# A new hand-written step list for the first two chunks of attention plus feed-forward on one NeuronCore

## The chip, the cores and the metric

The kernel runs on 1 core of a Trainium2 chip. The metric is the device time of one execution in microseconds (us); the median of 3 runs before the change is 620.47 (620.06 to 621.1). Engines are named as in the profile: PE (TensorE matmul), PEld (its weight loads), DVE (VectorE), ACT (ScalarE), POOL (GpSimd), SP (SyncE, which here issues all DMAs).

## The reference

```python
B, H, S, D = 4, 8, 768, 64; block, window = 32, 16; scale = 1 / sqrt(D)
k_sum = k.reshape(B, H, 24, 32, D).max(axis=3)
v_sum = v.reshape(B, H, 24, 32, D).mean(axis=3)
scores_l = where(|i - j| < window, scale * q @ k.T, -1e9)
scores_s = scale * q @ k_sum.T + log(block)
a = softmax(concat([scores_l, scores_s]))          # sum + 1e-9 in the denominator
x = (a @ concat([v, v_sum])) as (3072 tokens, 512)
out = square(relu(x @ w_in)) @ w_out               # w_in 512x2048, w_out 2048x512, float64 words
```

Each query sees 31 neighbours and 24 block summaries (largest key, mean value). The weights arrive as 64-bit floats and are made into 32-bit ones on the chip.

## The kernel before, in words

**Tiling.** 3072 tokens are 24 groups of 128 (six per batch entry) and 12 chunks of two groups. The 2048 hidden columns are 16 f tiles. Matmuls of the feed-forward use a reduced 32-bit format, and each operand is split into a high and a low part, so that one product is three matmuls (high x high, high x low, low x high).

**Two regimes.** Chunks 2 to 11 run through `slot`, a fixed pipeline over pairs of f tiles with attention of the next groups placed between. Chunks 0 and 1 run from `START`, a string of about 600 steps in one order, in which weights are still arriving and being converted. Each engine takes its own steps from that string in that order and waits where an operand is not ready; nothing reorders within an engine. The list ends with S7, and the first slot's matmul follows on PE.

**The steps** (number: group, f tile or unit; a suffix a, v or p names the engine ACT, DVE or POOL):

- L: a DMA. `kv` transposed keys of batch 0, `kw` transposed keys and values of batch 1, `q`, `k`, `v` per group, `w` a weight tile of 1 MB, `vn` plain values for the block means.
- KS, KT, VT: block maxima and means (DVE). PK: copies the key summaries behind a group's gathered keys (DVE). SV, VC: means of batch 0 by PE, copied into place.
- S g.half: scores (PE); TT g.head: scale, mask, maximum (DVE); E: exponential (ACT); NR g.half: `inverse`, two tiny DVE instructions; N: `norm` (DVE or POOL); T g.half: four transposes on PE; TC: their copy out; O g: `outputs`, weights times values (PE); XH and XL: high (ACT) and low part (DVE) of the result.
- HI (ACT), LO (ACT or DVE), SH (DVE), AD (POOL): from 64-bit words to a float; CA: its high part (ACT or DVE); SU: its low part (DVE or POOL).
- F1: 12 matmuls of 256 columns; RE: relu; SQ: high part of the square (ACT); MU, GL: square and its low part (DVE); F2: 6 matmuls of 512 columns; EV: eviction of an accumulated output.

**Order of chunks.** `units` lists the FFN work of the first regime as 32 units of one chunk and one f tile: chunk 0 with f 0 to 4, chunk 1 with f 0 to 10, chunk 0 with f 5 to 15, chunk 1 with f 11 to 15.

**Buffers.** Six PSUM banks: scores in 0 and 1 for groups below 6; `free` is a queue of banks 3, 4 and 5 for T and F1; O of groups 0 to 4 always uses bank 2 (`outputs`). SBUF has 17 rooms of 8 KB per partition (`room`), shared by raw weights, split weights, `vn` and the key tiles: 16 split tiles end up in 16 of them, and one is spare.

**Scores.** Groups 0 to 3 use `scores_kt` (transposed keys in SBUF, 8 matmuls for a pair of heads), the later ones `scores` (gathered keys with the summaries behind them, 4 matmuls).

Of the kernel before, what the change touches and what calls it, by code (L numbers as in the profile page):

```python
# [45 lines left out]
TC1.0a L:q4 VC1v HI0 L:q3 VC2v LO0a N1.1p TT2.1 O0 TT2.2 TT2.0 HI2 SH0 T1.1 LO2v XH0a AD0 TC1.1v E2.1 XL0v E2.0
TT2.6 HI3 O1 TT2.5 SH2 CA0a SH3 AD2 TT2.7 XH1a TT2.4 TT2.3 E2.7 XL1v E2.2 S3.0 SU0v CA2a S3.1 LO3v E2.3 F1.0
L:w8 E2.4 L:k4 SU2v E2.6 L:w6 F1.1 E2.5 AD3 NR2.0 RE0v HI4 NR2.1 F1.2 MU0 RE1v SQ0 N2.1p SQ1 GL0v RE2a MU1 F2.0
SQ2 CA3v LO4a GL1v SU3p L:w9 T2.1 MU2 L:v2 HI8 F2.1 TT3.6 L:w7 TT3.4 TT3.5 L:v3 TT3.7 E3.6 GL2v L:k5 E3.7 N2.0v
F1.3 L:q5 E3.5 SH4 L:w5 E3.4 SH8 T2.0 TC2.1a F2.2 AD4 RE3v TC2.0a NR3.1 SQ3 MU3 HI6 GL3v TT3.1 F2.3 N3.1p TT3.2  # L50
# [21 lines left out]
def attn_ffn_kernel(ctx: ExitStack, tc: tile.TileContext, q, k, kt, v, vt, v0, w, masks, ident, mean, out):  # L72
# [46 lines left out]
    def load_k(g):  # L119
        nc.sync.dma_start(out=k_sb[g % 2][:, 0:4], in_=k[g // NT, g % NT])  # L120
# [553 lines left out]
```

## Time and profile before

| what | value |
|---|---|
| median of 3 runs | 620.47 us (620.06 to 621.1) |
| the profiled execution | 621.07 us, span 619.3 us |
| PE, DVE, ACT, POOL busy | 96%, 63%, 44%, 16% of the span |
| mean granted clock of PE | 0.992 |
| end of the step list (first matmul of chunk 2) | 138.45 us |

A row of a timeline gives start and duration in us, engine, source line, operation, tiles, shapes and count, and in brackets the idle time before it with what ended it. "x8" stands for fp32 matmuls counted in two passes each. A row of stretches gives the stretch, its length, and then busy us and count of each engine.

### The profile page before, as it was taken

To read this page: it belongs to the slowest core of one execution; us is meant where nothing else is said; L and a number is where in the kernel's file an instruction comes from. 1 tells how busy PE (TensorE), PEld (TensorE's weight loads), DVE (VectorE), ACT (ScalarE), POOL (GpSimd) and SP (SyncE) were. 2 spreads that over 40 slices of the span, in tenths; PEclk is the share of its full clock that TensorE was granted. 3 is DMA by queue.
4 is the path that set the end of the run, shared out by engine and by line. 5 is a ranking of instruction groups with operands and counts; after the bars stand their busy time and mean duration, and the time that the engine had idled before them with its cause. 6 is when DMAs were issued, how large, how long until landed. Compare 5 with 4: busy or idle time off the path is not lost.

```text
span 619.3 us, 12979 instructions
## 1 busy us (share of the span) xinstructions
PE 596.7 (96%) x5216; PEld 538.7 (87%) x5216; DVE 391.9 (63%) x1073; ACT 270.3 (44%) x706; POOL 97.2 (16%) x83
## 2 busy tenths in 40 slices
...
GB/s 302 380 351 327 214 62 15 195 155 166 0 2 130 143 2 114 109 1 106 116 2 78 144 52 49 174 1 22 150 2 2 171 0 3 86 1 1 35 0 35
DMA packets 19852, 60.36 MB, mean 97 GB/s; under 512 B 2768, under 2 KB 2896, under 8 KB 17744
## 3 DMA queue, kind: packets, MB, share of 16 engines
...
q14 instruction: 19, 0.16, 0.1%
...
## 4 chain that ended last, share of the span: by engine, by line
PE 92%; DMA 3%; DVE 2%; ACT 1%; SPq 1%; issue 0%; POOL 0%; DVEq 0%; POOLq 0%
PE o_ps L398 42%; PE ph L357 40%; PE s_ps L249 3%; PE ph L327 3%; PE s_ps L357 2%; DMA w_raw<-in_w 2%; DMA q_sb<-in_q 1%; PE ph L306 1%; PE s_ps L265 1%; PE s_ps L327 1%; DVE w_sb L234 0%; PE o_ps L136 0%; ACT w_sb L113 0%; SPq L159 0%; SPq L117 0%
## 5 line engine op out<-in xcount | busy, mean ns | idle before, releaser
L357 PE MATMUL ph<-xh,w_sb 128*128 128x256 f32 x1448 | 256.2, 279 | 0.7 <-DVE xl L344 0.5
L398 PE MATMUL o_ps<-w_sb,gh 128*128 128x512 f32 x768 | 237.9, 391 | 0.0
L357 PEld LDWEIGHTS ph<-xh,w_sb 128*128 128x128 f32 x1448 | 225.8, 189 | 9.1 <-issue 1.6
L357 PE MATMUL ph<-xl,w_sb 128*128 128x256 f32 x724 | 201.2, 278 | 0.0
L398 PEld LDWEIGHTS o_ps<-w_sb,gh 128*128 128x128 f32 x768 | 137.1, 188 | 24.9 <-issue 0.2
L376 DVE TENSOR_TENSOR ph<-ph,r 128x512 f32<-128x512 f32 (+1 forms) x101 | 64.7, 642 | 143.4 <-ACT r L365 142.7
L398 PE MATMUL o_ps<-w_sb,gl 128*128 128x512 f32 x384 | 151.4, 394 | 0.8 <-DVE gl L379 0.8
L365 ACT ACTIVATE r<-ph 128x512 f32<-128x512 f32 (+1 forms) x91 | 51.7, 568 | 199.0 <-PE ph L357 198.8
L357 PEld LDWEIGHTS ph<-xl,w_sb 128*128 128x128 f32 x724 | 136.9, 189 | 0.0
L285 ACT ACTIVATE e_sb<-e_sb,nmx 128x120 f32<-128x120 f32 x192 | 73.7, 385 | 78.2 <-DVE nmx L277 78.2
L313 DVE STREAM_TRANSPOSE pT<-e_sb 32x256 f32<-32x256 f32 x216 | 94.1, 436 | 3.7 <-POOL e_sb L300 0.7
L300 POOL TENSOR_TENSOR e_sb<-e_sb,sm 128x480 f32<-128x480 f32 x43 | 43.3, 1011 | 324.8 <-DVE sm L295 179.4
L398 PEld LDWEIGHTS o_ps<-w_sb,gl 128*128 128x128 f32 x384 | 72.2, 188 | 15.6 <-DVE gl L379 1.3
L379 DVE TENSOR_TENSOR gl<-ph,gh 128x512 fp32r<-128x512 f32 (+1 forms) x101 | 64.2, 636 | 10.5 <-DVE ph L376 0.5
L371 ACT ACTIVATE gh<-r 128x512 fp32r<-128x512 f32 (+1 forms) x112 | 63.9, 571 | 9.3 <-DVE r L367 5.8
L277 DVE CUSTOM_DVE_ANT_0 e_sb<-s_ps,mask_sb 128x120 f32<-128x120 f32 x192 | 43.4, 277 | 5.2 <-PE s_ps L249 1.6
L227 POOL TENSOR_TENSOR w_raw<-w_raw 128x1024 int32<-128x1024 int32 x16 | 35.3, 2215 | 23.8 <-DVE w_raw L223 7.0
L285 ACT ACTIVATION_READ_ACCUMULATOR e_sb<-e_sb,nmx 128x1 f32 x192 | 36.0, 188 | 0.0
L344 DVE TENSOR_TENSOR xl<-ph,xh 128x512 fp32r<-128x512 f32 x19 | 13.1, 691 | 22.7 <-ACT xh L341 22.7
L294 DVE TENSOR_SCALAR sm<-sm 128x4 f32<-128x4 f32 x48 | 16.3, 339 | 14.8 <-ACT e_sb L285 14.8
L341 ACT CAST xh<-ph 128x512 fp32r<-128x512 f32 x19 | 11.1, 586 | 26.9 <-PE ph L327 26.9
L327 PEld LDWEIGHTS ph<-pT,v_sb 128*64 128x64 f32 x608 | 18.6, 138 | 3.9 <-issue 3.3
...
## 6 DMA issues: line engine op xcount, KB each, us to landing
...
```

The costliest lines, as they stand in the source:

```text
L227: nc.gpsimd.tensor_tensor(out=hi, in0=hi, in1=lo, op=ALU.add)
L277: nc.vector.tensor_tensor_reduce(out=e_sb[:, h, 0:NK], in0=s_ps[g][h % 2][:, h // 2, 0:NK], in1=m, scale=-scale, scalar=3.0e38, op0=ALU.ad ...
L285: nc.scalar.activation(e, e, AF.Exp, bias=nmx[half][:, i : i + 1], scale=-1.0, accum_out=sm[half][:, i : i + 1])
L300: eng.tensor_mul(out=e, in0=e, in1=sm[half].unsqueeze(2).to_broadcast([P, 4, NK]))
L313: nc.vector.transpose(out=pT[g % 2][j * 32 : j * 32 + 32, :, i * 32 : i * 32 + 32], in_=e_sb[i * 32 : i * 32 + 32, :, j * 32 : j * 32 + 32],)
L327: nc.tensor.matmul(xp[o : o + 64, h // 2, s * 64 : s * 64 + 64], lhsT=v_sb[g % 2][:, s, h * 64 : h * 64 + 64], rhs=pT[g % 2][:, h, s * 64 ...
L357: nc.tensor.matmul(ph, lhsT=w_sb[f][:, w, cc * P : (cc + 1) * P], rhs=x[c][:, cc, :], start=(n == 0), stop=(n == 3 * NC4 - 1))
L365: nc.scalar.activation(r, ph, AF.Relu)
L371: nc.scalar.activation(gh, r, AF.Square)
L376: nc.vector.tensor_mul(out=ph, in0=ph, in1=r)
L379: nc.vector.tensor_sub(out=gl, in0=ph, in1=gh.bitcast(F32))
L398: nc.tensor.matmul(o_ps[c][tt], lhsT=g_[:, ts_], rhs=w_sb[f][:, w, DM:], start=(first and n == 0), stop=(last and n == 2),)
```

## The change

Only the first regime changes, with three small edits that reach the slots too (the form of `inverse`, more buffers for the maxima, the layout in which v lies in memory).

- **The list** is new: other order of loads, groups and f tiles. Loads of the first keys begin with pairs 2 and 3, the mask and w0 come earlier, O1 comes before O0.
- **f tiles in pairs**: a unit is now one chunk and two f tiles (16 units; F1.i.0 and F1.i.1 fill the halves of one bank, then one RE, SQ, MU, GL of 512 columns, then F2.i.0 and F2.i.1). The order is chunk 0 tiles 0 to 3, chunk 1 tiles 0 to 7, chunk 0 tiles 4 to 15, chunk 1 tiles 8 to 15.
- **Banks**: `free` holds 2, 3, 4 and 5 and also serves O, which gives its bank back at XL.
- **High weights from high words**: AD writes the sum into the low word; CA reads the shifted high word, so it needs SH alone; SU subtracts CA's result from the sum.
- **Six groups on transposed keys**: S4 and S5 use `scores_kt`; k4, k5, PK4 and PK5 go. The DRAM array of k loses batch 0.
- **T5 becomes TU5**: group 5 is transposed by DVE in 32x32 blocks instead of by PE.

```diff
-FROM_KT = 4
+FROM_KT = 6
-L:kv0 L:kv1 L:q0 L:kv3 L:kv2 L:id L:mask L:v0 KS0 L:q1 L:w1 KS1 L:vn0 L:mean S0.0 L:vn1 KS3 KS2 TT0.3 S0.1 TT0.2
+L:kv2 L:kv3 L:kv0 L:q0 L:mask L:kv1 L:w0 L:id L:q1 L:mean KS3 L:vn1 L:vn0 KS2 KS0 S0.1 TT0.5 TT0.4 TT0.6 E0.4 TT0.7
...
-        nc.sync.dma_start(out=v_sb[g % 2][0:96], in_=v[g // NT, g % NT])
+        nc.sync.dma_start(out=v_sb[g % 2][0:96], in_=v[g // NT, g % NT].rearrange("s j c -> j s c"))
-        nc.gpsimd.tensor_tensor(out=hi, in0=hi, in1=lo, op=ALU.add)
+        nc.gpsimd.tensor_tensor(out=lo, in0=hi, in1=lo, op=ALU.add)
...
-        eng.tensor_sub(out=w_sb[f][:, 1], in0=words(f)[1].bitcast(F32), in1=w_sb[f][:, 0].bitcast(F32))
+        eng.tensor_sub(out=w_sb[f][:, 1], in0=words(f)[0].bitcast(F32), in1=w_sb[f][:, 0].bitcast(F32))
-            nmx[half] = work.tile([P, 4], F32, name="nmx", tag="nmx", bufs=3)
-            sm[half] = work.tile([P, 4], F32, name="sm", tag="sm", bufs=3)
+            nmx[half] = work.tile([P, 4], F32, name="nmx", tag="nmx", bufs=7)
+            sm[half] = work.tile([P, 4], F32, name="sm", tag="sm", bufs=7)
-        nc.vector.tensor_scalar_add(sm[half], sm[half], 1.0e-9)
+        nc.vector.scalar_tensor_tensor(
+            out=sm[half], in0=sm[half], scalar=1.0e-9, in1=sm[half], op0=ALU.add, op1=ALU.max
+        )
-        xp = bank[2 if g < FROM_PAIRS - 1 else free[0] if g < FROM_PAIRS else 5 - g % 2]
+        if g < FROM_PAIRS:
+            held["O", g] = free.pop(0)
+        xp = bank[held["O", g] if g < FROM_PAIRS else 5 - g % 2]
...
+        if g < FROM_PAIRS:
+            free.append(held.pop(("O", g)))          # at the end of low_x
...
-    units = [(0, f, 0, 5) for f in range(5)] + [(1, f, 0, 11) for f in range(11)]
-    units += [(0, f, 5, NF) for f in range(5, NF)] + [(1, f, 11, NF) for f in range(11, NF)]
+    units = [(0, f, 0, 2) for f in range(2)] + [(1, f, 0, 4) for f in range(4)]
+    units += [(0, f, 2, NF // 2) for f in range(2, NF // 2)] + [(1, f, 4, NF // 2) for f in range(4, NF // 2)]
...
-            held["F1", i] = free.pop(0)
-            ph_of[i] = ffn1(*units[i][:2], bank[held["F1", i]][:, 0:CT])
+            if j == 0:
+                held["F1", i] = free.pop(0)
+                ph_of[i] = bank[held["F1", i]]
+            c, f = units[i][:2]
+            ffn1(c, 2 * f + j, ph_of[i][:, j * CT : (j + 1) * CT])
+        elif op == "TU":
+            turn(i, 4 * j, 4 * j + 4)
```

**PE, from the outputs of groups 0 and 1 to the first F1.** Before, in its order (L327 is O, L306 a T, L265 scores on transposed keys, the first of its rows being S3):

```order
L327 MATMUL s_ps<-pT_80,v_sb_75 64x64 x16
L306 MATMUL s_ps<-id_sb,e_sb 128x128 x4
L327 MATMUL s_ps<-pT_81,v_sb_76 64x64 x16
L265 MATMUL s_ps<-kv,q_sb_78 64x96 x4
L265 MATMUL s_ps<-ksum_82,q_sb_78 64x24 x4
```

After (L331 is O, L262 the scores, L363 F1):

```order
L331 MATMUL s_ps<-pT_81,v_sb_76 64x64 x16
L331 MATMUL s_ps<-pT_80,v_sb_75 64x64 x16
L306 MATMUL ph<-id_sb,e_sb 128x128 x4
L262 MATMUL s_ps<-kv,q_sb_78 64x96 x4
L262 MATMUL s_ps<-ksum_82,q_sb_78 64x24 x4
```

O1 (`pT_81`) and O0 now stand side by side, and T2.1 comes ahead of S3 instead of behind the first F1s.

**DVE, from the first weight tiles to the low part of group 0.** Before (L223 SH, L217 LO, L113 TC, L344 XL, L234 SU, L294 and L295 NR, L277 TT), from SU0 on:

```order
L344 TENSOR_TENSOR xl<-s_ps,xh 128x4x128
L234 TENSOR_TENSOR w_sb<-w_raw,w_sb 128x1024
L217 TENSOR_SCALAR w_raw<-w_raw 128x1024
L234 TENSOR_TENSOR w_sb<-w_raw,w_sb 128x1024
L294 TENSOR_SCALAR sm<-sm 128x4
L295 RECIPROCAL sm<-sm 128x4
L367 TENSOR_SCALAR r<-ph 128x256
L294 TENSOR_SCALAR sm<-sm 128x4
```

After (L219 SH, L213 LO, L109 CA, L292 and L295 NR, L274 TT, L300 N, L348 XL):

```order
L219 TENSOR_SCALAR w_raw<-w_raw 128x1024
L213 TENSOR_SCALAR w_raw<-w_raw 128x1024
L109 CAST w_sb<-w_raw 128x1024
L292 SCALAR_TENSOR_TENSOR sm<-sm 128x4
L295 RECIPROCAL sm<-sm 128x4
L274 ISA e_sb,nmx<-s_ps,mask_sb 128x120
L274 ISA nmx 128x1
L300 TENSOR_TENSOR e_sb<-e_sb,sm 128x4x120
L274 ISA e_sb,nmx<-s_ps,mask_sb 128x120
L274 ISA nmx 128x1
L348 TENSOR_TENSOR xl<-s_ps,xh 128x4x128
L292 SCALAR_TENSOR_TENSOR sm<-sm 128x4
```

The steps of group 2 (both NR and both N) now stand between the weight steps of tile 1 and the low parts of groups 1 and 0, on which the first F1 waits; before, XL1 stood ahead of NR2.

**DVE, after the last weight step SU15.** Before (L376 MU, L379 GL, L167 KT, L172 and L175 VT, L113 a copy), at the list's end:

```order
L379 TENSOR_TENSOR gl<-s_ps,gh 128x256
L379 TENSOR_TENSOR gl<-ph,gh 128x256
L113 COPY pT_81<-ph 128x512
L167 TENSOR_REDUCE ksum_83<-kv 128x24
L113 COPY k_sb_73<-ksum_83 128x192
L172 TENSOR_REDUCE vsum<-kv 128x24
```

After (L382 MU, L385 GL, L313 the transposes TU5, L419 EV, L163 KT, L168 and L171 VT):

```order
L382 TENSOR_TENSOR ph<-ph,r 128x512
L313 STREAM_TRANSPOSE pT_81<-e_sb 32x8x32 x4
L385 TENSOR_TENSOR gl<-ph,gh 128x512
L163 TENSOR_REDUCE ksum_83<-kv 128x24
L168 TENSOR_REDUCE vsum<-kv 128x24
L171 TENSOR_SCALAR vsum<-vsum 128x24
L313 STREAM_TRANSPOSE pT_81<-e_sb 32x8x32 x4
```

Twelve block transposes stand between the squares of the last units, where a copy stood; the four KT and VT stay in that stretch.

85 lines of the change are left out of this document (45 added, 40 removed).

## The prediction

> **What bounds the kernel now.** I read the page first, then busy time by stretches, then each engine's timeline in the first 140 us, the only part in which the two step lists differ.
>
> ```profile
> span 619.3 us, 12979 instructions
> PE 596.7 (96%) x5216; PEld 538.7 (87%) x5216; DVE 391.9 (63%) x1073; ACT 270.3 (44%) x706; POOL 97.2 (16%) x83
> ```
> TensorE is busy for 96% of the span, so a change of order can only win back the other 22.6 us, or time at a low clock. The stretches say where that time lies (columns: busy us and count of PE, PEld, DVE, ACT, POOL, then granted clock, DMA share, GB/s):
>
> ```profile
> 7.00:23.20 16.20, 11.58 (x218) 9.74 (x219) 11.21 (x50) 8.59 (x36) 4.23 (x4) 1.00 1.03 354
> 23.20:30.00 6.80, 3.10 (x72) 2.38 (x70) 6.30 (x16) 5.48 (x10) 4.89 (x3) 0.97 1.01 413
> 30.00:40.30 10.30, 8.70 (x118) 8.49 (x119) 9.30 (x24) 7.43 (x18) 5.68 (x3) 0.52 1.03 412
> 40.30:138.40 98.10, 96.56 (x832) 85.96 (x831) 82.17 (x196) 66.51 (x141) 38.61 (x19) 1.00 0.51 166
> 138.40:619.30 480.90, 476.75 (x3987) 432.09 (x3980) 280.85 (x790) 181.03 (x502) 40.63 (x45) 1.00 0.18 62
> ```
> Up to 40 us TensorE idles or runs at half clock; from 40.3 to 138.4 it misses 1.5 us in 98.1; after 138.4 the slots of chunks 2 to 11 run, which the change leaves alone. So the change is worth the difference in when S7, the last step of the list, ends. The timeline of PE shows how the list starts and ends:
>
> ```profile
> 26.25 0.66 PE L306 MATMUL s_ps<-id_sb,e_sb 128*128 128x128 f32 x4 [0.22 <-POOL e_sb L300]
> 30.69 1.98 PE L327 MATMUL s_ps<-pT,v_sb 128*64 128x64 f32 x32 [3.79 <-DVE xl L344]
> 33.58 0.60 PE L265 MATMUL s_ps<-kv,q_sb 64*64 64x96 f32 x8 [0.91 <-DMA q_sb<-in_q]
> 35.85 0.58 PE L357 MATMUL ph<-xh,w_sb 128*128 128x256 f32 x1
> ...
> 135.07 1.25 PE L327 MATMUL ph<-pT,v_sb 128*64 128x64 f32 x32 [0.35 <-DVE pT L113]
> 138.45 0.50 PE L357 MATMUL ph<-xh,w_sb 128*128 128x256 f32 x2
> ```
> O1 waits 3.79 us for XL0, because both output steps use bank 2; the clock then falls to half (0.52 from 30.0 to 40.3). The first FFN matmul, F1.0, starts at 35.85 and the list ends at 138.45. From 35.85 to 40.3, 4.45 us at half clock cost 2.2 us, so F1.0 to S7 is 102.6 - 2.2 - 1.5 = 98.9 us of work at full clock.
>
> **The change: TensorE's work.** Prices, from start to start at full clock (timeline of PE):
>
> ```profile
> 23.58 0.40 PE L265 MATMUL s_ps<-kv,q_sb 64*64 64x96 f32 x8
> 24.27 0.45 PE L327 MATMUL s_ps<-pT,v_sb 128*64 128x64 f32 x8
> ...
> 54.01 0.60 PE L306 MATMUL ph<-id_sb,e_sb 128*128 128x128 f32 x4
> 54.54 1.05 PE L249 MATMUL s_ps<-k_sb,q_sb 64*64 64x120 f32 x32
> 55.52 1.15 PE L327 MATMUL s_ps<-pT,v_sb 128*64 128x64 f32 x32
> ...
> 63.56 0.39 PE L357 MATMUL ph<-xh,w_sb 128*128 128x256 f32 x2
> 64.92 0.62 PE L398 MATMUL o_ps<-w_sb,gh 128*128 128x512 f32 x2
> 66.30 0.39 PE L398 MATMUL o_ps<-w_sb,gh 128*128 128x512 f32 x1
> ```
> Half a tile's scores on transposed keys take 0.69 us (23.58 to 24.27), a whole tile's on gathered keys 0.98, a T 0.53, the matmuls of an F1 1.36, of an F2 1.38 (an F is 1.37). S4 and S5 on transposed keys add 2 x (1.38 - 0.98) = 0.8 us. T5.0 and T5.1 leave TensorE (-1.1); T2.0 and T2.1 now stand ahead of F1.0.0 (-1.1 behind it). F1.0.0 to S7 becomes 97.5 us. Pairing f tiles leaves these matmuls as they are.
>
> **Where F1.0.0 starts.** O takes a bank from the free list now, so O1 and O0 follow each other. The same scores, turns and means precede them, so I keep the old time: O0 began at 24.27. DVE then works through four TT, SH1, LO1, CA1, NR2.1, N2.1, XL1, NR2.0, N2.0, XL0, and F1.0.0 needs the last. The timelines of DVE and of POOL give the prices:
>
> ```profile
> 25.43 0.28 DVE L277 CUSTOM_DVE_ANT_0 e_sb<-s_ps,mask_sb 128x120 f32<-128x120 f32 x1
> 25.63 0.28 DVE L277 CUSTOM_DVE_ANT_0 e_sb<-s_ps,mask_sb 128x120 f32<-128x120 f32 x1
> 29.36 0.68 DVE L113 COPY pT<-s_ps 128x512 f32<-128x512 f32 x1
> 29.96 0.68 DVE L344 TENSOR_TENSOR xl<-s_ps,xh 128x512 fp32r<-128x512 f32 x1
> ...
> 35.67 1.22 DVE L234 TENSOR_TENSOR w_sb<-w_raw,w_sb 128x1024 fp32r<-128x1024 f32 x1
> 36.81 1.86 DVE L294 TENSOR_SCALAR sm<-sm 128x4 f32<-128x4 f32 x1
> 95.40 2.95 DVE L234 TENSOR_TENSOR w_sb<-w_raw,w_sb 128x1024 fp32r<-128x1024 f32 x1 [0.16 <-ACT w_sb L113]
> ```
> ```profile
> 35.84 2.81 POOL L227 TENSOR_TENSOR w_raw<-w_raw 128x1024 int32<-128x1024 int32 x1 [1.84 <-DVE w_raw L217]
> 95.37 1.89 POOL L227 TENSOR_TENSOR w_raw<-w_raw 128x1024 int32<-128x1024 int32 x1 [3.03 <-ACT w_sb L113]
> ```
> While POOL adds words (L227, 1.89 us), some DVE instructions stand still: the tiny L294 took 1.86 us until POOL's end at 38.65, and L234, which reads two tiles of SBUF, took 2.95 us instead of 1.22 until 1.1 us after POOL's end at 97.26. The new `inverse` reads `sm` twice from SBUF, so by the nearer row, L234, it is still held up. Lower bound: it runs through in some 0.35 us (my estimate, two instructions of 4 elements). From 25.2, where DVE took up group 2 before (25.43): four TT of 0.20 and three weight steps of 0.6 (nearest row: the copy at 29.36, 0.60 to the next start) end at 27.8; AD1 holds NR2.1 to 29.7, and SU1 on POOL (about 2.4, my estimate from AD's 1.89 and SU's two reads) holds N2.1 to 32.2; N2.1, XL1, NR2.0, N2.0, XL0 and a TT take 2.9: 35.1. If the inverse is never held, the same chain gives 33.9. The mask now comes earlier in SP's queue:
>
> ```profile
> 11.12 0.28 DVE L277 CUSTOM_DVE_ANT_0 e_sb<-s_ps,mask_sb 128x120 f32<-128x120 f32 x1 [0.29 <-DMA mask_sb<-in_masks]
> ```
> This saves at most 1 us at the first TT, and LO0, put ahead of NR0.0, can spend it again by waiting for w0. I take half: F1.0.0 at 34.5, bounds 32.9 and 35.1. The Trainium skill, "SBUF — State Buffer", section "Who interferes with whom", says a VectorE instruction with two SBUF inputs contends with a GpSimd instruction that reads SBUF; it speaks against the new form of the inverse, and the row at 95.40 agrees. By that rule alone the start is the 35.1 end; if it did not hold for four elements, the 33.9.
>
> **From F1.0.0 on.** Up to the first F2 the list is alternating: S4, F1.0.1, T3.1, O2, T3.0, F1.1.0, O3, each behind a DVE or ACT step of groups 2 and 3 (N3.1, TC2.0, SU2, TC3.0, GL0). Three waits of some 0.5 us each, as against 1.5 in all before, and a clock that may be low again for a part: I take 2.0 us, bounds 0.5 and 5 (the old 2.2 plus 2.8 for a second such stretch). TensorE's bound for the end of S7: 34.5 + 97.5 + 2.0 = 134.0.
>
> **The second bound: DVE and the weight tiles.** One spare room means that all four `kw` loads follow SU15, the last weight step.
>
> ```profile
> 34.00:112.00 78.00, 76.97 (x669) 69.00 (x663) 69.08 (x165) 63.28 (x135) 42.02 (x20) 0.96 0.55 183
> 112.00:138.45 26.45, 25.94 (x248) 23.21 (x247) 18.92 (x42) 7.49 (x18) 0.00 (x0) 1.00 0.52 172
> 105.02 1.23 DVE L234 TENSOR_TENSOR w_sb<-w_raw,w_sb 128x1024 fp32r<-128x1024 f32 x1
> 106.33 0.33 SPq L163 DMA_DIRECT2D kv<-in_kt  x1
> 129.31 0.34 SPq L163 DMA_DIRECT2D kv<-in_kt  x1
> ```
> ```profile
> L313 DVE STREAM_TRANSPOSE pT<-e_sb 32x256 f32<-32x256 f32 x27 | 11.8, 435 | 1.1 <-POOL e_sb L300 0.7
> L376 DVE TENSOR_TENSOR ph<-ph,r 128x256 f32<-128x256 f32 x21 | 8.9, 426 | 1.9 <-ACT r L365 1.6
> L376 DVE TENSOR_TENSOR ph<-ph,r 128x512 f32<-128x512 f32 x10 | 7.0, 700 | 16.4 <-ACT r L365 16.3
> L367 DVE TENSOR_SCALAR r<-ph 128x256 f32<-128x256 f32 x10 | 4.2, 422 | 2.7 <-PE ph L357 2.7
> ```
> SU15 ended at 106.2 and S7 32 us behind it, with four loads some 7.7 us apart between. DVE was busy 69.1 of 78 us from 34 to 112; to 106.2 about 64. The changes to that: a 512-wide MU or GL takes 0.70 us where two 256-wide ones take 0.85, so ten pairs give 20 x 0.15 = 3.0, of which I count 2.0 since durations overlap by some 0.08; eight of the ten RE go to ACT or are merged, -2.2 (two 512-wide ones stay, some 0.6 each); one SU more +1.1; three CA more +1.8 and two LO less -1.2 at 0.6. So 62 us; at DVE's old share of 89% it is 70 us, and from XL0's 34.5, SU15 ends at 104.5, less up to 3 where the inverse isn't held. I take 103. In the new list 20 F, O5, S6 and S7 follow the F1.11.1 that needs tile 15: 20 x 1.37 + 3.1 = 30.5; 103 + 30.5 = 133.5. The chain of `kw` loads ends within this: two are through by F2.10, and KT3 falls about 2 us ahead of S6.
>
> **Costed at nothing.** High weights from the high words: CA no longer waits for AD; SU still waits for both, so F1 gains nothing. Halved v descriptors and a smaller k array: DMA share in 112 to 138 us is 0.52, and no PE wait in the list ends on v (bounds -0.5 and +0.5). No loads of k4 and k5: weights come 2 us earlier while DMA is full, but ACT and DVE, not arrival, set SU. More nmx buffers: no wait on them shows. TU5 puts twelve transposes on DVE in the last 27 us, where it is idle for 7.5; 12 x 0.435 = 5.2, less a copy, fits. The inverse in the slots: their PE is 476.75 of 480.9 busy and waits elsewhere: 0.
>
> **Sum.** The two bounds meet, so I add 0.2 for steps on which now one, now the other is late: S7 ends at 134.2 instead of 138.45, 4.25 us less. The profiled execution has 621.07 us around its span of 619.3, the median of the runs is 620.47, 0.6 below; I take the gain from the median: 616.2.
>
> **Rivals.**
> (A) The clock stays up and the waits fall away. Idle ahead of T2.1 is about 27 to 30 us, shorter than the 3.79 that ended at half clock. Then F1.0.0 at 33.5, losses of 0.5, and SU15 at 100: 131.5 by one bound, 130.5 by the other, gain 7: 613.5. The Trainium skill, "TensorE: Matmul & The Clock Gate", Part 1, says the clock halves after an idle window of about 3.4 us that runs freely; the rows at 26.25 and 30.69 agree, and by it a 3.1 us gap would mostly keep the clock. Against A: DVE has 11% idle in which to hide POOL's holds.
> (B) The gain is eaten: SU15 comes at 106, as before, because the same 16 tiles bound DVE and ACT (63.28 of 78) whatever TensorE does. End 136.5 and waits of 1: 619.5, no change. For it: DVE's 69.08 of 78. Against: the old list spread the tiles' needs further.
> (C) Slower: DVE stands in order behind steps that TensorE delays (MU2 behind RE2a behind F1.2.1; RE5 behind F1.5.1) and the weight steps behind it come late. DVE's idle from 34 on was 8 us to SU15; with 15, SU15 is at 34.5 + 62 + 15 = 111.5, end 142, 624. It decides from SU15 at 108.
>
> **How the numbers follow.** Forecast 0.42 (614.5 to 618), A 0.22, B 0.23, C 0.13. About 0.2%, 1.24 us, is what a measurement here can tell. B's half below 619.2 counts as faster: faster 0.74, same 0.13, slower 0.13. The range leaves out most of C and the far end of A: 612.5 to 620.8; the forecast's own is 614.5 to 618.
>
> **What would show it.** Right: no wait of O0 for xl; F1.0.0's first matmul at 33 to 35; F2.0.0 about 11 us behind it; the last DVE `w_sb` subtraction ending at 101 to 105; the first slot matmul of chunk 2 near 134; the inverse still up to 1.9 us beside POOL. Wrong: a stretch of half clock past 45 us, waits of PE on `w_sb` between 55 and 100 us that sum to over 3 us, or a wait of S6 on `k_sb` after the last `kw` load.

## The result and the profile after

The changed kernel takes 624.19 us (median of 4 runs, 624.07 to 624.75), the kernel before, run beside it, 620.79 (620.06 to 621.62). The ratio is 1.0051, with a 95% interval of 1.0038 to 1.0063: the change makes the kernel 3.2 us slower, where 616.2 (612.5 to 620.8) was forecast. Two executions in a slower state, one of e3_sp (858 us, the profiled one) and one of e8_gnf_relief (998 us), are left out of all medians and ratios below.

The page of the changed kernel, its stretches (the same columns as in the prediction), and PE's timeline from the first scores to the first slot:

```profile
span 622.4 us, 13028 instructions
PE 595.1 (96%) x5272; PEld 537.1 (86%) x5272; DVE 398.8 (64%) x1044; ACT 264.3 (42%) x680; POOL 93.6 (15%) x82
```
```profile
23.20:38.79 15.59, 8.23 (x176) 7.21 (x177) 12.80 (x39) 9.46 (x27) 8.01 (x4) 0.75 0.81 283
38.79:141.55 102.76, 99.93 (x902) 88.87 (x901) 93.31 (x168) 63.72 (x117) 36.95 (x18) 0.99 0.48 176
```
```profile
8.05 0.60 PE L262 MATMUL s_ps<-kv,q_sb 64*64 64x96 f32 x8 [8.05 <-DMA q_sb<-in_q]
14.61 1.12 PE L306 MATMUL s_ps<-id_sb,e_sb 128*128 128x128 f32 x4 [2.88 <-POOL e_sb L300]
...
34.73 1.08 PE L306 MATMUL ph<-id_sb,e_sb 128*128 128x128 f32 x4 [5.83 <-DVE e_sb L300]
38.79 0.78 PE L363 MATMUL s_ps<-xh,w_sb 128*128 128x256 f32 x2
49.11 0.74 PE L409 MATMUL o_ps<-w_sb,gh 128*128 128x512 f32 x2
140.57 1.04 PE L246 MATMUL s_ps<-k_sb,q_sb 64*64 64x120 f32 x30 [0.24 <-DVE xl L348]
141.55 0.51 PE L363 MATMUL ph<-xh,w_sb 128*128 128x256 f32 x2
```

The 3.79 us that O1 waited for XL0 are gone, and a wait of 5.83 us of the first transpose of group 2 (T2.1) for its norm N2.1 stands there instead. F1.0.0 starts at 38.79 (before 35.85), and the list ends at 141.55 (before 138.45). The slots take 622.4 - 141.55 = 480.85 us, as before (619.3 - 138.45). So the whole loss lies in the list. From F1.0.0 to its end the two kernels need about the same (102.76 and 102.6): against the kernel before, the loss is the late start, and the gain that was forecast behind it did not come.

In that second part DVE is busier, 93.31 us of 102.76 (86.15 of 102.6 before), where it was forecast to have less to do. PE idles there for 2.83 us (102.76 - 99.93), in short waits:

```profile
PE ph L363 <- DVE gl L385: 1.1, 1, 1.1
PE ph L306 <- POOL e_sb L300: 0.7, 1, 0.7
PE s_ps L363 <- DVE w_sb L231: 0.5, 1, 0.5
```

### The profile page after: what moved, and what is told of

Same layout as the page of the kernel before. It is cut to its first block, busy times and chain, and to the rows that moved or that the text cites. A ratio compares the mean times of both kernels' runs of the same rounds, so it can differ in the third digit from the quotient of the medians.

```text
span 622.4 us, 13028 instructions
## 1 busy us (share of the span) xinstructions
PE 595.1 (96%) x5272; PEld 537.1 (86%) x5272; DVE 398.8 (64%) x1044; ACT 264.3 (42%) x680; POOL 93.6 (15%) x82
## 4 chain that ended last, share of the span: by engine, by line
PE 88%; DVE 5%; DMA 3%; ACT 2%; issue 1%; POOL 1%; SPq 0%; DVEq 0%; POOLq 0%; ACTq 0%
PE o_ps L409 40%; PE ph L363 38%; PE ph L331 3%; PE s_ps L246 2%; PE s_ps L363 2%; DMA v_sb<-in_v 2%; DVE w_sb L231 1%; PE s_ps L262 1%; DMA q_sb<-in_q 1%; ACT e_sb L282 1%; PE ph L306 1%; POOL e_sb L300 1%; DVE w_raw L219 1%; DVE sm L292 0%; DVE e_sb L300 0%
## 5 line engine op out<-in xcount | busy, mean ns | idle before, releaser
L363 PE MATMUL ph<-xh,w_sb 128*128 128x256 f32 x1408 | 247.3, 278 | 1.8 <-DVE gl L385 1.1
L363 PEld LDWEIGHTS ph<-xh,w_sb 128*128 128x128 f32 x1408 | 217.9, 188 | 10.5 <-DVE gl L385 1.9
L363 PE MATMUL ph<-xl,w_sb 128*128 128x256 f32 x704 | 194.9, 277 | 0.0
L382 DVE TENSOR_TENSOR ph<-ph,r 128x512 f32<-128x512 f32 x88 | 61.4, 698 | 142.7 <-ACT r L371 142.2
L371 ACT ACTIVATE r<-ph 128x512 f32<-128x512 f32 x85 | 50.5, 594 | 196.6 <-PE ph L363 193.2
L363 PEld LDWEIGHTS ph<-xl,w_sb 128*128 128x128 f32 x704 | 132.3, 188 | 0.0
L313 DVE STREAM_TRANSPOSE pT<-e_sb 32x256 f32<-32x256 f32 x228 | 99.4, 436 | 3.9 <-POOL e_sb L300 0.7
L300 POOL TENSOR_TENSOR e_sb<-e_sb,sm 128x480 f32<-128x480 f32 x43 | 43.1, 1006 | 323.8 <-DVE sm L295 181.1
L377 ACT ACTIVATE gh<-r 128x512 fp32r<-128x512 f32 x96 | 60.7, 632 | 20.5 <-PE o_ps L409 12.8
L385 DVE TENSOR_TENSOR gl<-ph,gh 128x512 fp32r<-128x512 f32 x88 | 60.8, 691 | 9.0 <-ACT gh L377 0.4
L274 DVE CUSTOM_DVE_ANT_0 e_sb<-s_ps,mask_sb 128x120 f32<-128x120 f32 x192 | 43.3, 277 | 5.6 <-PE s_ps L262 5.0
L224 POOL TENSOR_TENSOR w_raw<-w_raw 128x1024 int32<-128x1024 int32 x16 | 34.5, 2165 | 36.6 <-DVE w_raw L219 13.9
L348 DVE TENSOR_TENSOR xl<-ph,xh 128x512 fp32r<-128x512 f32 x20 | 13.7, 690 | 22.7 <-ACT xh L345 22.7
L292 DVE SCALAR_TENSOR_TENSOR sm<-sm 128x4 f32<-128x4 f32 x48 | 15.1, 314 | 17.2 <-ACT e_sb L282 17.2
L363 PE MATMUL s_ps<-xh,w_sb 128*128 128x256 f32 x128 | 24.6, 291 | 0.5 <-DVE w_sb L231 0.5
L231 DVE TENSOR_TENSOR w_sb<-w_raw,w_sb 128x1024 fp32r<-128x1024 f32 x13 | 22.0, 1695 | 1.7 <-ACT w_sb L109 1.3
```

The source lines that it names most:

```text
L224: nc.gpsimd.tensor_tensor(out=lo, in0=hi, in1=lo, op=ALU.add)
L231: eng.tensor_sub(out=w_sb[f][:, 1], in0=words(f)[0].bitcast(F32), in1=w_sb[f][:, 0].bitcast(F32))
L274: nc.vector.tensor_tensor_reduce(out=e_sb[:, h, 0:NK], in0=s_ps[g][h % 2][:, h // 2, 0:NK], in1=m, scale=-scale, scalar=3.0e38, op0=ALU.ad ...
L300: eng.tensor_mul(out=e, in0=e, in1=sm[half].unsqueeze(2).to_broadcast([P, 4, NK]))
L313: nc.vector.transpose(out=pT[g % 2][j * 32 : j * 32 + 32, :, i * 32 : i * 32 + 32], in_=e_sb[i * 32 : i * 32 + 32, :, j * 32 : j * 32 + 32],)
L363: nc.tensor.matmul(ph, lhsT=w_sb[f][:, w, cc * P : (cc + 1) * P], rhs=x[c][:, cc, :], start=(n == 0), stop=(n == 3 * NC4 - 1))
```

## What holds DVE up

The groups of DVE's instructions between the last step ahead of F1.0.0 (XL0) and the end of SU15, first of the kernel before (34.0 to 106.3 us), then of the changed one (36.9 to 110.1); after the bar busy time, and the mean ns of one:

```profile
L234 DVE TENSOR_TENSOR w_sb<-w_raw,w_sb 128x1024 fp32r<-128x1024 f32 x12 | 17.6, 1467 | 0.2 <-ACT w_sb L113 0.2
L223 DVE TENSOR_SCALAR w_raw<-w_raw 128x1024 int32<-128x1024 int32 x12 | 8.4, 724 | 0.1
L294 DVE TENSOR_SCALAR sm<-sm 128x4 f32<-128x4 f32 x7 | 5.2, 750 | 0.5 <-ACT e_sb L285 0.5
```
```profile
L231 DVE TENSOR_TENSOR w_sb<-w_raw,w_sb 128x1024 fp32r<-128x1024 f32 x13 | 22.0, 1695 | 1.7 <-ACT w_sb L109 1.3 <-POOL w_raw L224 0.2
L219 DVE TENSOR_SCALAR w_raw<-w_raw 128x1024 int32<-128x1024 int32 x14 | 13.4, 976 | 1.6 <-ACT w_raw L208 1.6
L109 DVE CAST w_sb<-w_raw 128x1024 fp32r<-128x1024 f32 x7 | 5.6, 797 | 0.1
L292 DVE SCALAR_TENSOR_TENSOR sm<-sm 128x4 f32<-128x4 f32 x5 | 2.7, 545 | 0.0
L300 DVE TENSOR_TENSOR e_sb<-e_sb,sm 128x480 f32<-128x480 f32 x1 | 1.8, 1766 | 0.0
```

What one takes without POOL beside it stands in DVE's timeline, next to what it takes with POOL; POOL's rows follow:

```profile
69.73 2.73 DVE L231 TENSOR_TENSOR w_sb<-w_raw,w_sb 128x1024 fp32r<-128x1024 f32 x1
75.52 0.69 DVE L219 TENSOR_SCALAR w_raw<-w_raw 128x1024 int32<-128x1024 int32 x1
76.85 2.39 DVE L219 TENSOR_SCALAR w_raw<-w_raw 128x1024 int32<-128x1024 int32 x1
82.06 1.21 DVE L231 TENSOR_TENSOR w_sb<-w_raw,w_sb 128x1024 fp32r<-128x1024 f32 x1
```
```profile
69.46 1.92 POOL L224 TENSOR_TENSOR w_raw<-w_raw 128x1024 int32<-128x1024 int32 x1 [1.29 <-ACT w_raw L215]
76.34 4.65 POOL L224 TENSOR_TENSOR w_raw<-w_raw 128x1024 int32<-128x1024 int32 x2 [4.96 <-DVE w_raw L219]
```

SU at 69.73 ends 1.1 us behind POOL's add, SH at 76.85 0.55 behind the first of two. The time lost beside POOL (the holds) is estimated as count times mean less the free duration: 1.22 for SU, 0.69 for SH and CA, 0.155 for NR, 0.655 for N (the last two as they measure where POOL's adds are cut short, below).

- Before: SU 12 x 0.247 = 3.0, SH 12 x 0.034 = 0.4, NR 7 x 0.595 = 4.2, and three LO 0.3: about 7.9 us.
- After: SU 13 x 0.475 = 6.2, SH 14 x 0.286 = 4.0, CA 7 x 0.107 = 0.75, NR 5 x 0.39 = 1.95, N 1.1: about 14.0 us.

The stretches themselves, before and after (DVE is the third pair of busy time and count):

```profile
34.00:106.30 72.30, 71.27 (x625) 63.55 (x619) 64.68 (x153) 60.87 (x129) 42.02 (x20) 0.96 0.56 187
```
```profile
36.90:110.10 73.20, 70.62 (x677) 63.19 (x671) 67.43 (x123) 57.62 (x105) 36.95 (x18) 0.97 0.47 177
```

DVE's busy time is 64.7 and 67.4 us. Without the holds it is 56.8 and 53.4: its own work fell by 3.4 us, more than the 2 forecast, and the holds grew by 6. Theory H is that this growth is what ate the forecast gain. It is a form of W, that DVE's weight steps set the end whatever F1.0.0 does; the rival, S (or P), is that TensorE's own row of work from a late F1.0.0 sets it.

## The experiments

Ratios are to the kernel before, run beside each; gains in time below are differences of ratios times 620.8 us. Start is the first scores matmul (it waits for q0), F2.0.0 the first matmul of the second layer, end the first slot's matmul; these and the other stages are from the one profiled execution of each kernel. Edits are to the changed kernel unless another is named.

| kernel | start | F1.0.0 | F2.0.0 | SU15 ends | end | median us | ratio (95%) |
|---|---|---|---|---|---|---|---|
| before | 7.26 | 35.85 | 41.95 | 106.25 | 138.45 | 620.79 | 1 |
| changed | 8.05 | 38.79 | 49.11 | 110.1 | 141.55 | 624.19 | 1.0051 (1.0038 to 1.0063) |
| e1_table | 7.03 | 36.47 | 46.95 | 107.9 | 139.70 | 627.62 | 1.0096 (1.0081 to 1.0111) |
| e2_normpool | 8.43 | 34.39 | 47.43 | 108.7 | 140.32 | 622.31 | 1.0019 (1.0009 to 1.0028) |
| e3_sp | | | | | | 624.72 | 1.0049 (1.0032 to 1.0066) |
| e4_three | 8.32 | 33.00 | 45.78 | 106.7 | 138.55 | 625.74 | 1.0079 (1.0056 to 1.0101) |
| e5_table_gap | 8.17 | 37.60 | 47.93 | 108.9 | 140.37 | 623.09 | 1.0035 (1.0023 to 1.0046) |
| e6_f1first | 7.68 | 30.76 | 47.49 | 108.4 | 139.22 | 622.17 | 1.0026 (1.0008 to 1.0044) |
| e7_gnf | 8.27 | 30.11 | 47.15 | 108.4 | 139.23 | 622.02 | 1.0017 (1.0001 to 1.0034) |
| e8_gnf_relief | 8.38 | 30.23 | 47.85 | 106.4 | 137.34 | 619.38 | 0.9973 (0.9959 to 0.9988) |
| e9_after_noadd | 7.92 | 35.41 | 45.57 | 102.0 | 134.15 | 617.76 | 0.9945 (0.9926 to 0.9965) |
| e10_before_noadd | 5.83 | 35.27 | 40.39 | 102.0 | 135.31 | 619.45 | 0.9976 (0.9962 to 0.9990) |
| e11_more | 7.69 | 28.76 | 46.20 | 105.3 | 136.11 | 618.05 | 0.9953 (0.9934 to 0.9972) |
| e12_relief_only | 7.70 | 38.43 | 48.79 | 107.4 | 138.99 | 622.08 | 1.0012 (1.0001 to 1.0024) |
| e13_swaps | 7.72 | 38.45 | 48.77 | 109.0 | 140.44 | 623.46 | 1.0043 (1.0029 to 1.0057) |
| e14_oldinv | 8.53 | 39.30 | 49.67 | 110.6 | 142.05 | 624.69 | 1.0055 (1.0040 to 1.0070) |
| e15_more_swaps | 7.39 | 28.48 | 46.03 | 105.0 | 135.84 | 618.82 | 0.9959 (0.9944 to 0.9973) |

The start differs by 1.5 us between executions that load q0 at the same place of the list, so differences of ends below that say little by themselves; the ratios of the medians decide.

F1.0.0 is a poor mark for the start. In e6, e7, e8, e11 and e15 it only changes places with T2.1, S3 and T2.0, which TensorE then still has to do behind it. From F2.0.0 on, all versions of the changed list give TensorE the same work (some 732 matmuls in each trace), so the time from F2.0.0 to the end is what can be compared: 92.44 us in the changed kernel. The forecast has F2.0.0 at 45.5 (34.5 and 11) and the end 88.7 us behind it. So of the 7.35 us by which the end was missed, 3.6 lie ahead of F2.0.0 and 3.7 behind it.

### How late F1.0.0 is, and what that costs

**e1_table, and e5_table_gap.** ACT's first rows, before and after, show the load of the function table that an exponential needs:

```profile
0.73 1.28 ACT L285 ACT_TABLE_LOAD   x1 [0.73 <-PEq L664]
```
```profile
10.07 1.28 ACT L282 ACT_TABLE_LOAD   x1 [10.07 <-DVE nmx L274]
11.37 0.40 ACT L282 ACTIVATE e_sb<-e_sb,nmx 128x120 f32<-128x120 f32 x1
```

In the new list it stands behind the first exponential's wait for a maximum, on the path to the first T. e1 and then e5:

```diff
+    nc.scalar.activation(const.tile([P, 1], F32, name="warm"), vsum[:, 0, 0:1], AF.Exp)
```
```diff
-    const.tile([P, 16], F32, name="gap")
+    gap = const.tile([P, 16], F32, name="gap")
+    nc.scalar.activation(gap[:, 0:1], vsum[:, 0, 0:1], AF.Exp)
```

> The changed kernel with one more instruction at the start: an exponential of one zero column on ACT, so that the 1.28 us load of its function table no longer stands behind the first wait for a maximum. Nothing else moves. Theory S (the loss lies ahead of the first F1 and what is won there comes through to the end): E0.4 starts at 10.1 instead of 11.4, the first T about 1.2 earlier, F1.0.0 near 37.6, end of the list near 140.4, time 1.2 us under the changed kernel (ratio to the kernel before near 1.003 instead of 1.005). Theory W (the weight tiles set the end, by DVE's steps up to SU15 at 110): F1.0.0 earlier all the same, but SU15 and the end of the list within 0.3 us of 110.1 and 141.55, and PE waits for w_sb, gl or xl instead; ratio 1.005.

> The changed kernel with the early table load again, but the exponential's result is written into an unused column of an SBUF tile that is there already (gap), so that no other tile moves by the new one. Theory A (the new tile moved those behind it, and the matmuls that stream the weights got 4 ns longer each in the slots): the slots take 480.9 us again instead of 485.2, the list ends near 139.7 to 140.4 as with the first version, time 1.0 to 1.8 us under the changed kernel (ratio 1.002 to 1.0035). Theory B (a table load or an exponential at the start itself slows what follows): slots 485 and ratio 1.009 as before.

In e1 the list ends 1.85 us earlier, a good half of it from the earlier start, but the kernel is 2.8 us slower: the slots take 625.0 - 139.70 = 485.3 us. In e5 they take 621.3 - 140.37 = 480.9, and the time falls by 1.0 us against the changed kernel (the intervals of the two ratios overlap; the executions themselves, 622.5 to 623.31 and 624.07 to 624.75, do not). Theory A holds, in that the tile and not the early table load makes the slots longer; e4, with the same tile, has slots of 485.25. The groups of PE in the slots, e1 and then e5, show where the 4.4 us are:

```profile
L410 PE MATMUL o_ps<-w_sb,gh 128*128 128x512 f32 x586 | 183.5, 394 | 0.0
L410 PE MATMUL o_ps<-w_sb,gl 128*128 128x512 f32 x294 | 117.1, 398 | 0.0
```
```profile
L410 PE MATMUL o_ps<-w_sb,gh 128*128 128x512 f32 x592 | 183.0, 390 | 0.0
L410 PE MATMUL o_ps<-w_sb,gl 128*128 128x512 f32 x296 | 116.6, 394 | 0.0
```

Each matmul that streams 512 columns of w_sb takes 4 ns longer where one 4-byte tile is added behind the constant ones. Some 960 such matmuls lie in the slots: 3.8 us. That the tile moves w_sb, and that the address of w_sb is what matters, is argued, not shown.

**e2_normpool** takes away what held up the norm that T2.1 waited for.

```diff
-NR2.1 AD1 ... N2.1v ... NR2.0 SU1p N2.0v
+NR2.1 N2.1p ... NR2.0 N2.0p AD1 SU1p
```

> The changed kernel with the norms of group 2 (N2.1 and N2.0) on POOL instead of DVE, and put ahead of AD1 and SU1 in POOL's order, so that nothing of POOL stands beside the inverse and the norm that T2.1 waits for. Theory S: T2.1 at 31.5 to 32.5 instead of 34.7, F1.0.0 at 35 to 36 instead of 38.8, time 2.5 to 3.5 us under the changed kernel (621 to 621.5 where it has 624.2, ratio near 1.000). Theory W: SU15 stays near 110, or comes later since AD1 and SU1 end some 3 us later, the end stays within 0.5 us: ratio 1.005.

F1.0.0 comes 4.4 us earlier, at 34.39 where the prediction had 34.5, but SU15 only 1.4 and the end 1.2. POOL's AD1 and SU1 run later: PE now waits 1.3 us for NR3 and 0.6 for SU1, so that F2.0.0 comes only 1.7 us earlier. The clock took a part too: O takes 3.50 us where the changed kernel has 2.08, at a granted clock of 0.56 (27.0 to 30.5 us), and from 42 to 44 the clock is 0.50 again. In time 2.0 us came, where theory S gave 2.5 to 3.5 and W nothing.

**e6_f1first** lets TensorE have F1.0.0 to do while N2.1 is held up.

```diff
-NR2.1 AD1 ... T2.1 XL1 ... XL0 T2.0 ... F1.0.0
+XL1 XL0 NR2.1 AD1 ... F1.0.0 T2.1 ... T2.0
```

> The changed kernel with F1.0.0 ahead of T2.1 on TensorE, and the low parts of x that it needs (XL1, XL0) ahead of NR2.1 on DVE. POOL still holds NR2.1 and N2.1 up (AD1, SU1), but TensorE has F1.0.0 to do meanwhile. Theory S: F1.0.0 at 31.5 to 32.5, T2.1 still at 34 to 35.5; what TensorE wins is the 1.4 us (2.7 at half clock) of F1.0.0 that now lies in the gap: time 1.3 to 2.7 us under the changed kernel (ratio 1.001 to 1.003). Theory W (DVE sets the end): its work and its holds are the same, SU15 within 0.5 of 110, and time within 0.5 us of the changed kernel (1.005).

F1.0.0 now starts 8 us earlier, F2.0.0 1.6, and the end moves by 2.3 (0.4 of it the start), the time by 1.6. That is within what theory S gave (1.3 to 2.7), and theory W misses: SU15 comes 1.7 us earlier, where it was to stay within 0.5. **e7_gnf** puts table load, norms and order together:

> Table load early without a new tile, norms of group 2 on POOL ahead of AD1, and F1.0.0 ahead of T2.1. Theory S: F1.0.0 near 31, list ends at 137 to 138.5, ratio 0.996 to 0.999. Theory W: as the early table load with the norms on POOL gave (list end 138.6): ratio 0.999 to 1.001, since F1.0.0's place is not what holds the end.

Its list ends at 139.23, no better than e6 and later than either theory had it (1.0017 in ratio; W gave 0.999 to 1.001, S less). It is 0.7 worse than that of **e4_three**, in which F1.0.0 stands 2.9 us later (e4 also has e3's earlier loads, and e1's extra tile, so its time is not to be used, its list is):

> The three edits together: early table load, norms of group 2 on POOL ahead of AD1, w3 and w5 ahead of q4 and v2. Theory S: the two gains ahead of F1.0.0 add, F1.0.0 at 34 to 35, time 4 to 4.5 us under the changed kernel: 619.7 to 620.2, ratio 0.998 to 1.000. Theory W: what the loads give and no more, ratio 1.000 to 1.005, with F1.0.0 early and PE idle between 45 and 110.

With F1.0.0 anywhere from 30.1 to 39.3 us, the time from F2.0.0 to the end stays at 91.7 to 92.9 us in the changed kernel and in e1, e2 and e4 to e7 (92.4 in e14 too). So what is won ahead of F2.0.0 comes through to the end, and none of these edits wins anything behind it. The late start is one part of the loss; it is not what makes the second part long.

**e3_sp** moves `L:w3 L:w5` ahead of `L:q4`. The table has its times only.

> The changed kernel with the loads of w3 and w5 issued ahead of q4 and v2, which wait on SP for S2.0 and O0 and left the DMA at 121 GB/s from 25 to 30 us. Theory S: w3 and w5 land 3 to 4 us earlier, but F1.0.0 needs neither, so it stays within 0.3 of 38.8 and the time within 0.5 us of the changed kernel (ratio 1.005). Theory W: earlier weights let their steps run earlier, SU15 comes 1 to 3 us earlier and so does the end (ratio 1.000 to 1.003).

No change (1.0049 against 1.0051): closing the gap in the DMA with these two loads wins nothing, which speaks against arrival of the weights as the cause.

### What sets the end

**e8_gnf_relief** and **e12_relief_only** rename four steps, in e7 and in the changed kernel:

```diff
-CA8v CA9v CA12v RE5v
+CA8a CA9a CA12a RE5a
```

> The kernel with the three edits (table, norms, F1.0.0 first), and four steps between 70 and 105 us on ACT instead of DVE: CA8, CA9, CA12 and RE5, about 2.5 us of DVE's time in a stretch where it is busy for 96 to 98%. Theory S (TensorE's own row of work sets the end, it idles for 0.8 us from 70 to 105): SU15 up to 2 us earlier, the end at most 0.8 us earlier. Theory W (DVE's weight steps set it): SU15 and the end 1.5 to 2.5 us earlier than with the three edits alone.

> The changed kernel with nothing but the four steps (CA8, CA9, CA12, RE5) on ACT instead of DVE. F1.0.0 stays at 38.8 and TensorE idles for 2.8 us from there to the end of the list, 1.9 of it after 70 us. Theory W (DVE's weight steps set the end by themselves): the end 1.5 to 2.5 us earlier as in the version with the early edits, ratio 1.001 to 1.003. Theory M (in the changed kernel both bounds meet, TensorE's from the late F1.0.0 and DVE's): 0.3 to 1.2 us, ratio 1.003 to 1.0045.

Both move SU15 and the end alike: by 2.0 and 1.9 us in e8 against e7, by 2.7 and 2.6 in e12 against the changed kernel, of which 0.35 is the start. In time e8 wins 2.7 us and e12 2.4. Theory W holds in both, and M falls: with F1.0.0 as late as 38.4, some 2.5 us less work on DVE (the estimate made ahead of e8) still comes out almost whole at the end. The stretches from F2.0.0 to the end, of the changed kernel, e12 and e9 (below), show it:

```profile
49.11:141.55 92.44, 89.62 (x732) 79.36 (x729) 83.17 (x135) 55.05 (x92) 32.17 (x15) 1.00 0.45 163
48.79:138.99 90.20, 88.73 (x732) 79.39 (x729) 78.60 (x131) 59.02 (x96) 32.14 (x15) 1.00 0.47 167
45.57:134.15 88.58, 88.33 (x733) 79.60 (x729) 73.20 (x135) 55.12 (x92) 10.29 (x15) 1.00 0.51 183
```

Here the relief takes 2.2 us off, and 2.6 in e8 against e7 (92.08 and 89.49). Behind F2.0.0 it is DVE that sets the end.

**e9_after_noadd** and **e10_before_noadd** cut POOL's adds, in the changed kernel and in the one before:

```diff
-        nc.gpsimd.tensor_tensor(out=lo, in0=hi, in1=lo, op=ALU.add)
+        nc.gpsimd.tensor_tensor(out=lo[:, 0:8], in0=hi[:, 0:8], in1=lo[:, 0:8], op=ALU.add)
```

> The changed kernel with the add of the weight words on POOL cut to 8 of 1024 columns (the weights are then wrong; all other steps and waits stay), so that POOL no longer stands beside DVE. Theory H (DVE's instructions stand still for 14.3 us beside POOL between XL0 and SU15, against 8.0 in the kernel before, and this is where the saving forecast for DVE went): SU15 comes 6 to 10 us earlier, at 100 to 104, and the list ends at 133 to 136, close to the 134.2 of the prediction; 5 to 8 us under the changed kernel; the gain is at least 2 us larger than the same cut gives the kernel before. Theory P (TensorE's own row from a late F1.0.0 sets the end): F1.0.0 comes some 2 to 3 us earlier since nothing holds NR2.1, the end as much and no more, about 138.5 to 139.5.

> The kernel before with the same cut of POOL's add to 8 of 1024 columns (weights wrong in the same way). Theory H: DVE loses 8.0 us of holds less, SU15 3 to 6 us earlier, the list ends 2 to 4.5 us earlier (134 to 136.5), so that the order of the two kernels turns round: the changed one is 1 to 4 us faster without the adds. Theory P: F1.0 and the end both 1 to 2 us earlier, and the changed kernel stays slower by 2 us or more.

Without the adds the changed kernel has SU15 at 102.0 and the end at 134.15, where the prediction had 103 and 134.2; it gains 6.6 us in time, the kernel before 1.5 (its end, 3.1 us earlier, has 1.4 from an early q0). Theory H holds in both. The order turns round: 617.76 against 619.45. DVE's groups in e9, 34.0 to 102.1 us:

```profile
L231 DVE TENSOR_TENSOR w_sb<-w_raw,w_sb 128x1024 fp32r<-128x1024 f32 x13 | 16.8, 1295 | 1.9 <-ACT w_sb L109 1.7
L219 DVE TENSOR_SCALAR w_raw<-w_raw 128x1024 int32<-128x1024 int32 x14 | 10.8, 781 | 1.8 <-ACT w_raw L208 1.6
L292 DVE SCALAR_TENSOR_TENSOR sm<-sm 128x4 f32<-128x4 f32 x5 | 0.8, 155 | 0.0
```

The same 13 SU take 16.8 us instead of 22.0, the same 14 SH 10.8 instead of 13.4. Between the same two steps (XL0 and SU15) DVE is busy for 57.2 us in e10 and 56.0 in e9, 7.5 and 11.3 less than with the adds. By this measure the holds beside the adds grew by 3.8 us from one kernel to the other; the sums above, which take in POOL's other steps, have 6.

Of the 7.4 us by which e9's list ends earlier, 3.5 lie ahead of F2.0.0 and 3.9 behind it. Both parts come to where the forecast had them: F2.0.0 at 45.57 (45.5), the rest 88.58 us (88.7). Ahead of F2.0.0 not all is holds: N2.1 ends 1.55 us earlier since AD1 no longer holds NR2.1 up, and then the clock is at 1.00 from 32 us on, where the changed kernel had 0.50 until 41. Behind F2.0.0 TensorE idles for 0.25 us in e9, so there its own row of work sets the end. The cut also takes away POOL's time for the adds; but DVE had waited for an add for only 0.2 us, so the 3.9 us are put down to the holds.

### Why the holds grew

**e13_swaps** changes only DVE's order, so that instructions that read PSUM stand beside the adds. POOL does not hold these up: MU and GL take 0.69 us each in the changed kernel and in e9.

```diff
-SU6v SH11 MU4 ... SH8 CA8v SH10 TC4.0v GL4 ... SU9v MU6 ... SH13 SH14 SU12v
+MU4 SU6v SH11 ... SH10 SH8 TC4.0v GL4 CA8v ... MU6 SU9v ... SU12v SH14 SH13
```

> The changed kernel with six moves on DVE between 68 and 101 us and nothing on another engine: MU4 ahead of SU6, MU6 ahead of SU9, SU12 ahead of SH13 and SH14 with SH14 ahead of SH13, SH10 ahead of SH8, TC4.0 and GL4 ahead of CA8. Each puts an instruction that POOL does not hold up (it reads PSUM) beside an add, where one that POOL holds up stood. The same work, the same instructions. Theory O (the order beside POOL's adds makes the growth of the holds, from 8.0 to 14.3 us): holds 3 to 4 us less, SU15 1.5 to 4 us earlier, the end 1 to 2 us earlier, ratio 1.002 to 1.0035. Theory K (the kind of the work makes it: more instructions that can be held, less of the others, so that POOL's 27 us of adds meet a held one in any order): holds and end within 0.5 us, ratio 1.0045 to 1.0055.

Between both theories. SU's mean fell, CA's rose:

```profile
L231 DVE TENSOR_TENSOR w_sb<-w_raw,w_sb 128x1024 fp32r<-128x1024 f32 x13 | 19.8, 1532 | 1.5 <-ACT w_sb L109 1.3
L219 DVE TENSOR_SCALAR w_raw<-w_raw 128x1024 int32<-128x1024 int32 x14 | 13.1, 956 | 1.6 <-ACT w_raw L208 1.6
L109 DVE CAST w_sb<-w_raw 128x1024 fp32r<-128x1024 f32 x7 | 6.3, 898 | 0.0
```

By the same sum the holds are SU 4.1, SH 3.7, CA 1.5, NR and N 3.05: 12.3 us, 1.7 less, and the end comes 0.8 us earlier when the start is taken off. The interval of the time (1.0029 to 1.0057) takes in no change. So these six moves take off 1.7 us of holds, of 6 that grew; a part only went from SU to CA. The rest fits the kind of work, which is argued and not shown: MU, GL and RE, which read PSUM and which POOL leaves alone, fell from 21.9 us to 15.0 in the two stretches (sums over their groups in the view of DVE's instructions above), while SU went from 12 to 13, SH from 12 to 14 and CA from 4 to 7. More instructions that can be held, and fewer others to lay beside the adds; how much each is worth was not tried.

**e14_oldinv** puts `tensor_scalar_add` back in `inverse`.

> The changed kernel with the inverse in its old form, one add of a constant (one input from SBUF) instead of the instruction that names the same input twice. Theory R (the hold beside POOL does not ask for two inputs from SBUF: the old form stood 1.86 us in the kernel before): the sum of its rows stays at 15 to 16 us, the time within 0.5 us of the changed kernel, ratio 1.0045 to 1.0055. Theory N (the new form is held more than the old one): NR2.1 takes 0.2 us instead of 1.42, T2.1 stays at 34.7 since SU1 holds N2.1 to then; the later ones win 1 to 2 us of DVE, ratio 1.002 to 1.004.

Theory R holds: 1.0055, and the rows of the whole execution, changed kernel first, are alike:

```profile
L292 DVE SCALAR_TENSOR_TENSOR sm<-sm 128x4 f32<-128x4 f32 x48 | 15.1, 314 | 17.2 <-ACT e_sb L282 17.2
```
```profile
L292 DVE TENSOR_SCALAR sm<-sm 128x4 f32<-128x4 f32 x48 | 15.5, 324 | 17.0 <-ACT e_sb L282 17.0
```

The Trainium skill, "SBUF — State Buffer", section "Who interferes with whom", says besides the rule on two SBUF inputs that copy, cast and tensor_scalar can enter a mode in which they contend with GpSimd too. The rows of SH (a tensor_scalar, 2.39 us instead of 0.69), of CA (a cast, 1.46 us at 95.15, beside the add at 94.16) and of the old inverse agree.

### A version that beats both

**e11_more** is e8 with further steps:

```diff
-VC0v VC1a VC2v VC3a TC1.1a ... SU1p ... CA7v ... RE9v
+VC0a VC1a VC2a VC3a TC1.1v ... SU1v (ahead of SH2) ... CA7a ... RE9a
```

> The version with table, norms, F1.0.0 first and four steps moved from DVE to ACT, and further: the four copies of the means all on ACT and TC1.1 on DVE, SU1 on DVE ahead of SH2 instead of on POOL, RE9 and CA7 on ACT. Theory W (DVE still sets the end): SU15 1 to 2 us earlier than the 106.4 without these, end 0.5 to 1.5 us under 137.3, ratio 0.995 to 0.9965. Theory S (TensorE is without a gap from 45 us on in that version, so only its start and its clock can still give): the end moves by what F1.0.0 to F2.0.0 moves, less than 0.5 us; ratio 0.9965 to 0.998.

It takes 618.05 us, 2.9 less than the kernel before (0.9953). SU15 and the end move by about as much (1.1 and 1.2 us), 0.7 of which is the start; the interval takes in both theories. **e15_more_swaps** adds e13's moves:

> The best version so far (618.05 us: table, norms on POOL, F1.0.0 first, means on ACT, SU1 on DVE, six steps moved to ACT) with the same six moves on DVE. TensorE has hardly a gap behind 50 us there, so theory S gives no change (ratio 0.994 to 0.9965, end within 0.5 of 136.1). Theory W, DVE still sets the end: 0.7 to 1.5 us earlier, ratio 0.9925 to 0.994.

No change (0.9959 against 0.9953, the ends 0.3 apart with a start 0.3 earlier). From F2.0.0 to the end DVE is busy for 74.18 us instead of 75.93, so the moves did take off 1.75 us, and the stretch stays as it is (89.81 and 89.91). Theory S holds here: in this version DVE no longer sets the end.

## Why the prediction was wrong

Two terms of the sum failed: the start of F1.0.0 in the first bound, and DVE's busy time in the second. Parted at F2.0.0, each makes about half of the miss.

**TensorE's bound (134.0).** The step that failed is the start: F1.0.0 was put at 34.5 and came at 38.79. Without the 2.83 us that TensorE idles behind it, its own row would have ended at 138.7, no earlier than in the kernel before. The rows of PE, of DVE and of the clock:

```profile
26.82 2.08 PE L331 MATMUL s_ps<-pT,v_sb 128*64 128x64 f32 x64
```
```profile
30.21 1.42 DVE L292 SCALAR_TENSOR_TENSOR sm<-sm 128x4 f32<-128x4 f32 x1 [0.35 <-ACT e_sb L282]
31.93 2.66 DVE L300 TENSOR_TENSOR e_sb<-e_sb,sm 128x480 f32<-128x480 f32 x1
...
36.33 0.68 DVE L348 TENSOR_TENSOR xl<-s_ps,xh 128x512 fp32r<-128x512 f32 x1
```
```profile
40.00:41.00 1.00, 1.00 (x6) 1.00 (x6) 0.97 (x6) 1.00 (x7) 0.19 (x1) 0.50 1.06 426
41.00:42.00 1.00, 1.00 (x33) 0.87 (x34) 1.00 (x2) 1.00 (x7) 1.00 (x1) 0.89 0.99 401
```

Of the 4.3 us, 2.5 were lost ahead of O, which began at 26.82: I kept its old start of 24.27 since the same steps precede it, but the table load of 1.28 us had come onto the path (e5 wins 1.0 back) and q0 came 0.8 later. That load stood at 0.73 us in the profile before, hidden, and I passed it by. From O on, DVE's chain was held up as the 35.1 bound had it (NR2.1 1.42 us by AD1, N2.1 2.66 by SU1), and XL0 ended at 37.0. F1.0.0 came 1.8 us behind, since PE had T2.1, S3 and T2.0 ahead of it and ran them at half clock, 4.06 us from 34.73 on (e9, at full clock, does the same in 2.2); these I had not priced. The work from F1.0.0 on: 102.76 less 2.83 us idle (102.76 - 99.93) and 1.3 for the half clock up to 41.3 is 98.6, where I had 97.5; the losses of 4.1 lie within their bounds of 0.5 to 5.

**DVE's bound (133.5).** This was the bound that decided, 141.55 against 138.7, as e8, e12 and e9 show. The step that failed is its busy time to SU15: 62 us forecast, 67.4 measured. I corrected the old busy time by counts at durations of some 0.6 to 1.1 us, those without POOL (1.1 for an SU, 0.6 for a CA), and carried the old holds over unchanged inside it. An SU took 1.70, an SH 0.98, and the holds went from 7.9 to 14.0 us. The count was off too: two more SH fall into the stretch (12 before, 14 after), some 1.4 us at 0.69 each, and the terms as written add up to 61.5, not 62. The row with the price of a hold (2.95 us at 95.40) stood in my own text, and I used it only on the way to F1.0.0. From XL0's later end (2.4 us), 5.4 us more busy time, 2.2 less idle and the 1.5 that I took off, SU15 came 7.1 us late, and from there to the end it took 31.5 us where I had 30.5.

**What was right.** O no longer waits for XL0; F2.0.0 follows F1.0.0 by 10.3 us; the inverse stands up to 1.86 us beside POOL; the slots did not change; no half clock past 45 us, no 3 us of waits on w_sb, no wait of S6 on k_sb. None of the signs that I named for a wrong forecast came, since I had named none for the holds; of the signs for a right one, F1.0.0, SU15 and the end all missed. The chance of faster was also added up wrongly: 0.42, 0.22 and half of 0.23 are 0.755, not 0.74.

**The rivals.** C's figures came (SU15 at 108 or later, 624), not its reason: DVE was to idle 15 us behind steps that TensorE delays, and idled 5.8 (73.2 - 67.4). A's clock fell to half all the same. B's reason, that the same 16 tiles bound DVE whatever TensorE does, is borne out behind F2.0.0 only, where 92 us stay 92 however early F2.0.0 is; its SU15 at 106 came at 110.1.

**Costed at nothing.** The new inverse is worth nothing either way (e14), the slots kept their 480.85 us, and weights that come earlier win nothing (e3). The single effects of the high words, v's descriptors, the buffers for the maxima and TU5 were not tried.
